# Capped attention, routed experts and a dense layer on one core: cap's terms and the guard's exponential in other places, fewer filling products, and the last tokens' output in two halves of columns

## The chip, the cores and the metric

The kernel runs on one core of a Trainium2 chip. Five engines matter, each with its own queue of instructions, which it works through in order: TensorE (PE) multiplies matrices, VectorE (DVE) and ScalarE (ACT) work on columns, GpSimd (POOL) builds tables and issues indirect DMAs, and SyncE (SP) issues the other DMAs. The engines wait for each other by semaphores. The metric is the device time of one execution in microseconds (us).

## The reference

Three stages follow one another: attention with capped scores, a layer in which each token goes to one of eight experts, and a dense layer with SiLU.

```python
def _attn_ref(q, k, v, cap):                 # 2 batches, 12 heads, 448 tokens, 64 wide
    scores = scale * np.matmul(q, k.transpose(0, 1, 3, 2))
    scores = cap * np.tanh(scores / cap)     # cap = 30
    scores = scores - np.max(scores, axis=-1, keepdims=True)
    attn = np.exp(scores)
    attn = attn / (np.sum(attn, axis=-1, keepdims=True) + 1e-09)
    return np.matmul(attn, v)
...
    logits = x @ w_gate + modality_bias[modality_id]      # 896 tokens, 768 wide, 8 experts
    e_idx = np.argmax(logits, axis=1)
...
        h = np.maximum(x[mask] @ w1[e], 0.0)              # 768 -> 1024
        out[mask] = gate_w[mask, None] * (h @ w2[e])      # 1024 -> 768
...
    h = x @ w_in                                          # 768 -> 2048
    g = h * (1.0 / (1.0 + np.exp(-h)))
    return g @ w_out                                      # 2048 -> 768
```

## The kernel before

**Precision.** Operands of the exact products are split into a high part (fp32r) and the rest, and three products (high by high, rest by high, high by rest) make one. `parts(j)` makes the splits of q and k on DVE.

**Attention.** Heads are worked in 12 pairs. For a pair, `scores(j)` makes the transposed scores in three chunks of 128 keys for both heads and one shared chunk of the last 64 keys of each; ACT takes the tanh out of PSUM (line 339, scaled by `tscale`, which is 0.125 / cap) and then the exp (line 342, scaled by cap). The values of the pair before are multiplied in between (line 402), and their result is copied out of PSUM by ACT (line 412). The row sums are added on DVE (lines 375, 376), moved across partitions by four DMAs on SP's queue (line 385) and folded (lines 391, 392). In the first two pairs, when PE would have nothing to do, `warm(n)` issues n filling products of a zero tile (line 365).

**Cap's terms.** `cap_terms` makes 1/cap, `tscale` (line 187) and an exponent for the guard (line 188) on DVE and issues the DMA of the gate weights on ACT's queue; `cap_guard` makes a flag for a slow path (lines 192, 194) and the guard itself, by an exp of one column on ACT (line 195) and a product on DVE (line 196). The guard is what the softmax adds to its sum; it is first used when pair 0's rows are normalised. Before, both stand behind pair 0's splits and ahead of pair 1's.

**ACT's function table.** The build places an ACT_TABLE_LOAD ahead of the first ACTIVATE whose function is not loaded; one load serves both tanh and exp, and a second comes before SiLU.

**Experts and last layer.** Tokens are sorted by expert, and two experts' weights stream through. The last layer runs in four quarters `q` of the 2048 hidden columns: first the products into the hidden columns (line 1170, SiLU on ACT), then, for seven groups `s` of 128 sorted tokens, 24 products of 128x384 into the 768 output columns (line 1200). For the first five groups the quarters are added up in SBUF (line 1215). The last two groups keep their sums in PSUM through all quarters, one bank for each half of 384 columns; at the end ACT copies one half (line 1210) and DVE the other (line 1211). In the last quarter each group is written by an indirect DMA on POOL's queue (line 1217), with the token rows in `ordr`. The table behind `ordr` is itself made by eight indirect writes (line 892).

**Order.** The code issues each engine's instructions in the order in which it is written (a manual schedule); the framework adds the semaphore waits. `hooks` names what runs after the scores of a pair: 0 is behind pair 0.

Of the kernel before, what the change touches and what calls it, by code (L numbers as in the profile page):

```python
# [13 lines left out]
I32 = mybir.dt.int32  # L14
AF = mybir.ActivationFunctionType
ALU = mybir.AluOpType
# [5 lines left out]
NT, DM, E, FF, DFF = 896, 768, 8, 1024, 2048  # L22
# [10 lines left out]
NQ = 4  # L33
FQ = NFF // NQ
# [28 lines left out]
def moe_stack_kernel(ctx, tc, qT, kT, va, cap, mid, wg, wgb, mb, w1, w2, w_in, w_out, out):  # L63
# [120 lines left out]
    def cap_terms():  # L184
        A.dma_start(out=wg_sb, in_=wgb)
        V.reciprocal(rcap, capt)
        V.tensor_scalar_mul(tscale, rcap, 0.125)
        V.scalar_tensor_tensor(guard, in0=capt, scalar=-1.0, in1=capt, op0=ALU.mult, op1=ALU.min)

    def cap_guard():  # L190
        big = small([1, 1])
        V.tensor_scalar(big, guard[0:1], -CAPMAX, None, op0=ALU.is_lt)
        st["big"], st["slow"] = big, small([1, 1], I32)
        V.tensor_copy(st["slow"], big)
        A.activation(guard, guard, AF.Exp)
        V.tensor_scalar_mul(guard, guard, 1.0e-9)
# [80 lines left out]
    def attention(ap, psa, hooks):  # L277
# [21 lines left out]
        def parts(j):  # L299

            qh, kh = qk["q2", j], qk["k2", j]
            q1 = ap.tile([128, S], F32R, tag="q1", name="q1", bufs=3)
            q3 = ap.tile([128, S], F32R, tag="q3", name="q3", bufs=3)
            k1 = ap.tile([128, KW], F32R, tag="k1", name="k1", bufs=3)
            k3 = ap.tile([128, KW], F32R, tag="k3", name="k3", bufs=3)
            split_t[j] = (q1, q3, k1, k3)

            def first(ks):
                V.tensor_copy(k1[:, ks], kh[:, ks])
                V.tensor_copy(q1, qh)  # L310
                V.tensor_sub(k3[:, ks], kh[:, ks], f32(k1[:, ks]))
                V.tensor_sub(q3, qh, f32(q1[:]))

            if j == 0:
                first(slice(0, 2 * KC))
                V.tensor_copy(k1[:, 2 * KC:], kh[:, 2 * KC:])
                V.tensor_sub(k3[:, 2 * KC:], kh[:, 2 * KC:], f32(k1[:, 2 * KC:]))
            else:
                first(slice(0, KW))
# [161 lines left out]
        load_v(0)  # L481
        load(1)
        parts(0)
        cap_terms()
        cap_guard()
        load(2)
        parts(1)
        for j in range(NP + 2):
            if j + 3 < NP:
                load(j + 3)  # L490
            if j + 1 < NP:
                load_v(j + 1)

            def between():
                if j == NP + 1:
                    warm(6, banks2())
                if j > 1 and not moved(j - 2):
                    rows_of(j - 2)
                if j == 0:
                    warm(8)  # L500
                if j == 1:
                    warm(8)
                if 0 < j <= NP:
                    values(j - 1)
                    evict(j - 1)
                if j == NP:
                    fold(j - 2)
                if 0 < j <= NP:
                    sums(j - 1)
                if j > 1 and j != NP:  # L510
                    fold(j - 2)

            if j < NP:
                scores(j, between)
            else:
                between()
            if j + 2 < NP:
                parts(j + 2)
            for f in hooks.get(2 * j, ()):
                f()  # L520
            if j > 1 and moved(j - 2):
                rows_of(j - 2)
            for f in hooks.get(2 * j + 1, ()):
                f()
# [461 lines left out]
    with (  # L986
        tc.tile_pool(name="attn", bufs=2) as ap,
        tc.tile_pool(name="ps2a", bufs=2, space=PSUM) as ps[2],
        tc.tile_pool(name="psa", bufs=1, space=PSUM) as ps[0],
    ):  # L990
        for _ in range(NWARM):
            T.matmul(bank(), lhsT=wb[:, :128], rhs=wb, start=True, stop=True)
        hooks = {
            0: [setup],
            H + 3: [lambda: choose(0)],
            H + 5: [
                lambda: place(0), lambda: weigh(0, 0), plan_experts, lambda: weigh(0, 1), plan_windows
            ],
            H + 7: [early_window, take_windows, lambda: stream.load(2)],
            H + 8: [do("A", "find", NC), do("A", "gather", 0), do("A", "gather", 1)],  # L1000
            H + 9: [lambda: stream.load(4)],
            H + 10: [do("A", "scale", 0), do("A", "scale", 1), do("A", "flip_both", 0), do("A", "flip_both", 1)],
            H + 11: [lambda: stream.split(1), lambda: stream.load(NLOAD)],
            H + 13: [late_window, lambda: stream.split(2), lambda: stream.load(NF)],
            H + 14: [take_columns],
        }
        attention(ap, ps[0], hooks)
        weigh(1)
# [3 lines left out]
    with tc.tile_pool(name="late", bufs=1) as late:  # L1012
# [142 lines left out]
        osum = late.tile([128, NT // 128, DM], F32, tag="r1", name="osum")  # L1155
        sums = {s: (bank(), bank()) for s in range(NT // 128 - 2, NT // 128)}
        ordr = mo.tile([128, NT // 128, 2], I32, name="ordr")
        for q in range(NQ):
            gs = late.tile([128, 2, FQ, NT], F32R, tag="big", name="gs")
            for fi in range(FQ):  # L1160
                n = 2 * FQ * q + fi
                feed(2 * FQ * q + (4, 5, 6, 8)[fi], 2 * FQ * q + (6, 7, 8, 8)[fi])
                wh, wl = wide.get(n)
                p = banks2()
                i = 0
                for d in range(ND):
                    cs = slice(d * 128, (d + 1) * 128)
                    for w_, x_ in ((wh, 0), (wh, 1), (wl, 0)):
                        for half in range(2):
                            T.matmul(  # L1170
                                p[:, half, :S],
                                lhsT=w_[:, cs],
                                rhs=ys[:, x_, d, half * S:(half + 1) * S],
                                start=(i == 0),
                                stop=(i == 3 * ND - 1),
                            )
                        i += 1
                sg = mo.tile([128, 2, S], F32, tag="tmp", name="sg")
                A.activation(sg, p[:, :, :S], AF.Silu)  # L1179
                sf = sg.rearrange("p a s -> p (a s)")  # L1180
                A.copy(gs[:, 0, fi, :], sf)  # L1181
                V.tensor_sub(gs[:, 1, fi, :], sf, f32(gs[:, 0, fi, :]))  # L1182
            if q == 0:
                plan_order()
                G.dma_start(out=ordr, in_=order.rearrange("(s p) f -> p s f", p=128))
            n = 2 * FQ * q + FQ
            for s in range(NT // 128):
                feed(n + FQ + (0, 0, 0, 1, 1, 2, 2)[s], n + FQ + (0, 1, 2, 2, 3, 3, 4)[s])
                ss = slice(s * 128, (s + 1) * 128)
                held = s in sums  # L1190
                if held:
                    ph = [x[:, :384] for x in sums[s]]
                else:
                    p = banks2()
                    ph = [p[:, half, :384] for half in range(2)]
                for fi in range(FQ):
                    hi, lo = wide.get(n + fi)
                    for i, (g_, w_) in enumerate(((0, hi), (0, lo), (1, hi))):
                        for half in range(2):
                            T.matmul(  # L1200
                                ph[half],
                                lhsT=gs[:, g_, fi, ss],
                                rhs=w_[:, half * 384:(half + 1) * 384],
                                start=(fi == 0 and i == 0 and (q == 0 or not held)),
                                stop=(fi == FQ - 1 and i == 2 and (q == NQ - 1 or not held)),
                            )
                osl = osum[:, s, :].rearrange("p (a c) -> p a c", a=2)
                if held:
                    if q == NQ - 1:
                        A.copy(osl[:, 0], ph[0])  # L1210
                        V.tensor_copy(osl[:, 1], ph[1])  # L1211
                elif q == 0:
                    A.copy(osl, p[:, :, :384])
                else:
                    V.tensor_tensor(out=osl, in0=osl, in1=p[:, :, :384], op=ALU.add)
                if q == NQ - 1:
                    G.indirect_dma_start(  # L1217
                        out=out, out_offset=IOA(ap=ordr[:, s, 0:1], axis=0), in_=osum[:, s, :], in_offset=None
                    )


_OUTS = [((896, 768), "float32")]
# [61 lines left out]
```

## Time and profile before

| | before |
|---|---|
| median of 3 runs | 503.33 us (499.53 to 504.95) |
| the profiled execution, its time | 505.51 us |
| its span, first to last instruction | 503.8 us |
| its mean granted TensorE clock | 0.974 of full speed |
| PE busy | 485.6 us (96%) |
| DVE busy | 322.7 us (64%) |
| ACT busy | 230.9 us (46%) |
| POOL busy | 67.8 us (13%) |

The profile is one execution. Its views show instructions with start and duration in us from the span's start, what ended the idle time before them (in brackets), the time from a DMA's issue to its landing, and in stretches of time the busy time of each engine with the granted TensorE clock, 1.00 for 2.4 GHz and 0.50 for 1.2 GHz. Names left of an arrow are written, names right of it are read; `sc`, `sh`, `p`, `xv` and `out` are accumulators in PSUM.

### The profile page before, as it was taken

To read this page: it belongs to the slowest core of one execution; us is meant where nothing else is said; L and a number is where in the kernel's file an instruction comes from. 1 tells how busy PE (TensorE), PEld (TensorE's weight loads), DVE (VectorE), ACT (ScalarE), POOL (GpSimd) and SP (SyncE) were. 2 spreads that over 40 slices of the span, in tenths; PEclk is the share of its full clock that TensorE was granted. 3 is DMA by queue.
4 is the path that set the end of the run, shared out by engine and by line. 5 is a ranking of instruction groups with operands and counts; after the bars stand their busy time and mean duration, and the time that the engine had idled before them with its cause. 6 is when DMAs were issued, how large, how long until landed. Compare 5 with 4: busy or idle time off the path is not lost.

```text
span 503.8 us, 7670 instructions
## 1 busy us (share of the span) xinstructions
PE 485.6 (96%) x2975; PEld 417.6 (83%) x2975; DVE 322.7 (64%) x554; ACT 230.9 (46%) x275; POOL 67.8 (13%) x151
## 2 busy tenths in 40 slices
PE   8999999989889999999999999999999999999994
PEld 4465666549779988888889999999999999999994
DVE  6679887787647354484777845764877647876220
ACT  5899996921444444243435543354224441235100
POOL 6400006201273300000000011121000000000121
PEclk9999997979789999999999999999999999999999
DMA  7566652832523344735113406685225214340022
GB/s 192 167 172 178 207 168 70 286 89 79 173 74 96 89 119 131 249 134 182 62 64 115 133 6 129 131 125 118 87 103 165 86 62 127 126 126 0 33 94 94
DMA packets 21486, 60.99 MB, mean 121 GB/s; under 512 B 4081, under 2 KB 8689, under 8 KB 21441
## 3 DMA queue, kind: packets, MB, share of 16 engines
q1 hardware_dynamic: 17920, 51.62, 35.6%
q0 software_dynamic: 3088, 8.54, 5.1%
q8 instruction: 25, 0.41, 0.3%
q10 hardware_dynamic: 432, 0.25, 0.2%
q14 instruction: 21, 0.16, 0.1%
HBM read 49.84 MB, written 5.52 MB: 110 GB/s over the span
## 4 chain that ended last, share of the span: by engine, by line
PE 59%; POOLq 0%; issue 0%; DVE 0%
PE sc L1170 23%; PE sc L1200 17%; PE p L1200 7%; PE p L732 6%; PE p L759 6%; POOLq L1280 0%; DVE osum L1211 0%; POOLq L1217 0%
## 5 line engine op out<-in xcount | busy, mean ns | idle before, releaser
L1170 PE MATMUL sc<-ys,hi 128*128 128x448 f32 x384 | 94.4, 368 | 0.0
L1170 PEld LDWEIGHTS sc<-ys,hi 128*128 128x128 f32 x384 | 72.0, 188 | 6.7
L1200 PE MATMUL sc<-hi,gs 128*128 128x384 f32 x320 | 69.1, 336 | 0.0
L1200 PEld LDWEIGHTS sc<-hi,gs 128*128 128x128 f32 x320 | 56.8, 188 | 0.1
L1170 PE MATMUL sc<-ys,lo 128*128 128x448 f32 x192 | 55.0, 367 | 0.0
L125 ACT ACTIVATE w<-raw 128x768 f32<-128x768 f32 x32 | 28.5, 897 | 53.4 <-DVE lo L150 53.4
L759 PE MATMUL p<-r,hi 128*128 128x464 f32 x176 | 51.9, 376 | 0.0
L402 PE MATMUL xv<-at,vx 128*64 128x448 f32 x192 | 43.4, 599 | 0.0
L732 PE MATMUL p<-r,hi 128*128 128x464 f32 (+1 forms) x168 | 41.0, 334 | 0.4 <-PEq L1080 0.4
L1200 PE MATMUL sc<-lo,gs 128*128 128x384 f32 x160 | 40.8, 336 | 0.0
L342 ACT ACTIVATE at<-th,c 128x1344 f32<-128x1344 f32 (+2 forms) x25 | 38.8, 1552 | 0.8
L1170 PEld LDWEIGHTS sc<-ys,lo 128*128 128x128 f32 x192 | 36.0, 188 | 3.4
L339 ACT ACTIVATE th<-sc,c 128x896 f32<-128x896 f32 x36 | 35.1, 1004 | 4.6 <-PE sc L328 4.2
L1182 DVE TENSOR_TENSOR gs<-sg,gs 128x896 fp32r<-128x896 f32 x16 | 17.5, 1092 | 30.8 <-ACT gs L1181 30.8
L759 PEld LDWEIGHTS p<-r,hi 128*128 128x128 f32 x176 | 32.7, 188 | 4.1
L1179 ACT ACTIVATE sg<-sc 128x896 f32<-128x896 f32 x16 | 14.7, 921 | 41.3 <-PE sc L1170 41.3
L149 ACT CAST hi<-w 128x768 fp32r<-128x768 f32 x32 | 26.2, 830 | 16.0 <-DVE w L131 9.4
L402 PEld LDWEIGHTS xv<-at,vx 128*64 128x64 f32 x192 | 13.8, 149 | 23.5 <-issue 22.9
L736 ACT ACTIVATE r<-p 128x256 fp32r<-128x256 f32 (+2 forms) x24 | 10.5, 443 | 49.5 <-PE p L732 35.8
L126 DVE TENSOR_SCALAR w<-w 128x768 f32<-128x768 f32 x32 | 17.9, 558 | 23.9 <-ACT w L125 23.6
L759 PE MATMUL p<-r,lo 128*128 128x464 f32 x88 | 32.9, 374 | 0.0
L328 PE MATMUL sc<-q,k 64*128 64x448 f32 x216 | 30.2, 405 | 2.0 <-ACT th L339 1.9
(237 smaller groups left out, 871.6 us busy)
## 6 DMA issues: line engine op xcount, KB each, us to landing
raw<-in_w_dram SPq DMA_DIRECT2D x32, 384.0 KB, 4.0
raw<-in_w_in_dram SPq DMA_DIRECT2D x16, 768.0 KB, 4.7
raw<-in_w_out_dram SPq DMA_DIRECT2D x16, 768.0 KB, 4.4
gf<-gh SPq DMA_DIRECT2D x44, 112.0 KB, 2.3
vx<-in_va_dram SPq DMA_DIRECT2D x12, 256.0 KB, 4.1
k<-in_kT_dram SPq DMA_DIRECT2D x11, 256.0 KB, 2.9
xd<-xt POOLq DMA_DIRECT2D x6, 448.0 KB, 4.1
q<-in_qT_dram SPq DMA_DIRECT2D x11, 224.0 KB, 2.9
```

The costliest lines, as they stand in the source:

```text
L125: A.activation(w.bitcast(F32), top.bitcast(F32), AF.Abs)
L126: V.tensor_scalar(w.bitcast(F32), w.bitcast(F32), MIN_TOP, None, op0=ALU.max)
L149: A.copy(hi, x)
L328: T.matmul(out[:, :S], lhsT=k_[rows, c * KC:(c + 1) * KC], rhs=q_[rows], start=(i == 0), stop=(i == 2))
L339: A.activation(th[:, c:c + n], p, AF.Tanh, scale=tscale)
L342: A.activation(at[:, c:c + n], th[:, c:c + n], AF.Exp, scale=capt)
L402: T.matmul(p[own, :S], lhsT=vx[:, c * KC + r * D:c * KC + (r + 1) * D], rhs=at[:, 2 * c + r if c < NK else 2 * NK, :], start=(c == 0), sto ...
L732: T.matmul(p[:, :n], lhsT=w_[:, cs], rhs=xs[x_][:, d, :], start=(i == 0), stop=(i == 3 * ND - 1))
L759: T.matmul(p[:, :n], lhsT=w_[:, cs], rhs=hs[h_][:, f, :n], start=(i == 0), stop=(i == 3 * NF - 1))
L1170: T.matmul(p[:, half, :S], lhsT=w_[:, cs], rhs=ys[:, x_, d, half * S:(half + 1) * S], start=(i == 0), stop=(i == 3 * ND - 1),)
L1182: V.tensor_sub(gs[:, 1, fi, :], sf, f32(gs[:, 0, fi, :]))
L1200: T.matmul(ph[half], lhsT=gs[:, g_, fi, ss], rhs=w_[:, half * 384:(half + 1) * 384], start=(fi == 0 and i == 0 and (q == 0 or not held)), ...
```

## The change

Four edits. `cap_terms` moves into `parts(0)`, between the splits that the first two chunks of scores need and those of the other half of k. `cap_guard` moves to the hook behind pair 0's scores, ahead of `setup`. Pair 1's filling products are six instead of eight. The seventh group of tokens makes its 24 products by halves of columns: 12 into the first half, then copies of 192 columns by ACT and by DVE and an indirect write of that half, then the same for the second. The output is seen as 1792 rows of 384 for this, and `ordh` holds the doubled row numbers, made on DVE in quarter 1.

```diff
@@ parts @@
             if j == 0:
                 first(slice(0, 2 * KC))
+                cap_terms()
                 V.tensor_copy(k1[:, 2 * KC:], kh[:, 2 * KC:])
                 V.tensor_sub(k3[:, 2 * KC:], kh[:, 2 * KC:], f32(k1[:, 2 * KC:]))
@@ attention @@
         parts(0)
-        cap_terms()
-        cap_guard()
         load(2)
...
                 if j == 1:
-                    warm(8)
+                    warm(6)
...
         hooks = {
-            0: [setup],
+            0: [cap_guard, setup],
...
+        ordh = mo.tile([128, 2], I32, name="ordh")
...
+            if q == 1:
+
+                V.tensor_scalar(ordh[:, 0:1], ordr[:, NT // 128 - 1, 0:1], 1, None, op0=ALU.logical_shift_left)
+                V.tensor_scalar(ordh[:, 1:2], ordh[:, 0:1], 1, None, op0=ALU.bitwise_or)
...
+                def products(halves):
+                    for fi in range(FQ):
+                        hi, lo = wide.get(n + fi)
+                        for i, (g_, w_) in enumerate(((0, hi), (0, lo), (1, hi))):
+                            for half in halves:
+                                T.matmul(
...
+                def write(to, row, x):
+                    G.indirect_dma_start(out=to, out_offset=IOA(ap=row, axis=0), in_=x, in_offset=None)
+
+                if s == NT // 128 - 1 and last:
+
+                    for half in range(2):
+                        products((half,))
+                        A.copy(osl[:, half, :192], ph[half][:, :192])
+                        V.tensor_copy(osl[:, half, 192:], ph[half][:, 192:])
+                        write(
+                            out.rearrange("t (a c) -> (t a) c", a=2), ordh[:, half:half + 1], osl[:, half]
+                        )
+                    continue
+                products(range(2))
...
                 if q == NQ - 1:
-                    G.indirect_dma_start(
-                        out=out, out_offset=IOA(ap=ordr[:, s, 0:1], axis=0), in_=osum[:, s, :], in_offset=None
-                    )
+                    write(out, ordr[:, s, 0:1], osum[:, s, :])
```

**The order on ACT at the start.** Before, from the first DMA of q to the second tanh; `c` are cap's terms, in brackets the semaphores that each instruction waits for.

```order
L290 DMA q_119<-in_qT_dram 128x448
L292 DMA c_71<-in_cap_dram 128x1
L185 DMA wg_sb<-in_wgb_dram 128x48
L195 ACT_TABLE_LOAD
L195 ACTIVATE c_74<-c_74 128x1 [waits DVE_49]
L339 ACTIVATE th<-sc,c_73 128x896 [waits PE_49]
L342 ACTIVATE at<-th,c_71 128x896 [waits DMAHW3_49,Activation_49]
```

The same place on ACT in the changed program, down to the guard's exp (L195; lines from 314 on are one higher).

```order
L290 DMA q_119<-in_qT_dram 128x448
L292 DMA c_71<-in_cap_dram 128x1
L185 DMA wg_sb<-in_wgb_dram 128x48
L340 ACT_TABLE_LOAD [waits DVE_49]
L340 ACTIVATE th<-sc,c_73 128x896 [waits PE_49]
L343 ACTIVATE at<-th,c_71 128x896 [waits DMAHW3_49,Activation_49]
L340 ACTIVATE th<-sc,c_73 128x896 [waits PE_49]
L343 ACTIVATE at<-th,c_71 128x896 [waits Activation_49]
L340 ACTIVATE th<-sh,c_73 128x448 [waits PE_49]
L340 ACTIVATE th<-sc,c_73 128x896 [waits PE_49]
L343 ACTIVATE at<-th,c_71 128x1344 [waits Activation_49]
L195 ACTIVATE c_74<-c_74 128x1 [waits DVE_49]
```

The guard's exp stands behind pair 0's last exp, and the table load belongs to the first tanh and carries a wait for DVE.

**The order on DVE at the start.** Before, from the last split that pair 0's first chunks need.

```order
L312 TENSOR_TENSOR q_131<-q_119,q_130 128x448 [waits DVE_49]
L316 CAST k_132<-k_118 128x256 [waits DMAHW2_49]
L317 TENSOR_TENSOR k_133<-k_118,k_132 128x256 [waits DVE_49]
L186 RECIPROCAL c_72<-c_71 128x1 [waits DMAHW3_49]
L187 TENSOR_SCALAR c_73<-c_72 128x1 [waits DVE_49]
L188 SCALAR_TENSOR_TENSOR c_74<-c_71 128x1
L192 TENSOR_SCALAR c_144<-c_74 1x1 [waits DVE_49]
L194 CAST c_146<-c_144 1x1 [waits DVE_49]
L196 TENSOR_SCALAR c_74<-c_74 128x1 [waits Activation_49]
```

The same engine in the changed program, a little later: from the end of pair 2's splits to pair 0's sums (L376).

```order
L312 TENSOR_TENSOR q_206<-q_146,q_205 128x448 [waits DVE_49]
L192 TENSOR_SCALAR c_213<-c_74 1x1
L194 CAST c_215<-c_213 1x1 [waits DVE_49]
L196 TENSOR_SCALAR c_74<-c_74 128x1 [waits Activation_49]
L252 TENSOR_SCALAR c_266<-c_265 112x8 [waits Pool_49]
L253 CAST vals<-c_266 112x8 [waits DVE_49]
L252 TENSOR_SCALAR c_266<-c_265 112x8 [waits DVE_49]
L253 CAST vals<-c_266 112x8 [waits DVE_49]
L254 MEMSET vals 112x8
L376 TENSOR_TENSOR gh<-at 128x896
```

Lines 192 to 196 stood right behind cap's terms and now stand behind pair 2's splits; lines 186 to 188 stand directly behind the first L312, ahead of the second half of k.

**The order on POOL at the end.** Before, the writes of the last five groups of tokens; DMASW are the semaphores that tell of the landing of POOL's DMAs, one after another in turn.

```order
L1217 DMA out_dram<-osum,ordr 896x768 [waits DMASW7_49,DVE_49]
L1217 DMA out_dram<-osum,ordr 896x768 [waits DMASW0_49,DVE_49]
L1217 DMA out_dram<-osum,ordr 896x768 [waits DMASW1_49,DVE_49]
L1217 DMA out_dram<-osum,ordr 896x768 [waits DMASW2_49,DVE_49,Activation_49]
L1217 DMA out_dram<-osum,ordr 896x768 [waits DMASW3_49,DVE_49,Activation_49]
```

The changed program, from the third group on.

```order
L1217 DMA out_dram<-osum,ordr 896x768 [waits DMASW7_49,DVE_49]
L1217 DMA out_dram<-osum,ordr 896x768 [waits DMASW0_49,DVE_49]
L1217 DMA out_dram<-osum,ordr 896x768 [waits DMASW1_49,DVE_49]
L1217 DMA out_dram<-osum,ordr 896x768 [waits DMASW2_49,DVE_49,Activation_49]
L1217 DMA out_dram<-osum,ordh 1792x384 [waits DMASW3_49,DVE_49]
L1217 DMA out_dram<-osum,ordh 1792x384 [waits DMASW4_49,DVE_49]
```

The last write has become two of half the columns, and the turn of landing semaphores goes on by one through both.

## Rows read from the trace of the kernel before

**Rows 1.** Chain of waits on the page, shares of the span by line.

```profile
PE sc L1170 23%; PE sc L1200 17%; PE p L1200 7%; PE p L732 6%; PE p L759 6%; POOLq L1280 0%; DVE osum L1211 0%; POOLq L1217 0%
```

**Rows 2.** Timeline of ACT from 0 (start, duration, instruction, [idle before <- releaser]).

```profile
1.24 0.46 ACTq L292 DMA_DIRECT2D c<-in_cap_dram  x1
...
2.22 1.28 ACT L195 ACT_TABLE_LOAD   x1 [2.22 <-issue]
7.28 0.20 ACT L195 ACTIVATE c<-c 128x1 f32<-128x1 f32 x1 [3.78 <-DVE c L192]
7.39 0.99 ACT L339 ACTIVATE th<-sc,c 128x896 f32<-128x896 f32 x1
...
16.27 1.79 ACT L342 ACTIVATE at<-th,c 128x1792 f32<-128x1792 f32 x1
18.83 0.54 ACT L412 COPY xs<-xv 128x448 f32<-128x448 f32 x1 [0.77 <-PE xv L402]
```

**Rows 3.** Timeline of the last 10 us, DVE's last instruction.

```profile
497.14 0.56 DVE L1211 COPY osum<-p 128x384 f32<-128x384 f32 x1 [3.60 <-PE p L1200]
```

**Rows 4.** Timeline of POOL: an order write, the last two output writes.

```profile
299.75 0.98 POOL L892 DMA_INDIRECT order<-ent,order  x1 [2.70 <-DMA order<-ent,order]
...
494.31 0.97 POOL L1217 DMA_INDIRECT out_dram<-osum,ordr  x1 [3.29 <-DVE osum L1211]
498.47 0.97 POOL L1217 DMA_INDIRECT out_dram<-osum,ordr  x1 [3.20 <-DVE osum L1211]
```

**Rows 5.** The output tensor's instructions, the seven writes' time from issue to landing.

```profile
DMA to landing us min/median/max: 3.0/3.0/3.1
```

**Rows 6.** Timeline of DVE in the first 24 us.

```profile
6.00 0.28 DVE L316 CAST k<-k 128x256 fp32r<-128x256 f32 x1
...
6.66 0.16 DVE L186 RECIPROCAL c<-c 128x1 f32<-128x1 f32 x1
6.85 0.15 DVE L187 TENSOR_SCALAR c<-c 128x1 f32<-128x1 f32 x1
...
7.11 0.14 DVE L192 TENSOR_SCALAR c<-c 1x1 f32<-1x1 f32 x1
...
13.58 1.08 DVE L375 TENSOR_TENSOR gh<-at 128x896 f32<-128x896 f32 x1
...
22.93 1.09 DVE L376 TENSOR_TENSOR gh<-gh,at 128x896 f32<-128x896 f32 x1 [3.69 <-ACT at L342]
23.93 0.62 DVE L391 TENSOR_TENSOR gf<-gf,at 128x448 f32<-128x448 f32 x1
```

**Rows 7.** DMA issues: queue, count, KB, us from issue to landing.

```profile
c<-in_cap_dram ACTq DMA_DIRECT2D x1, 0.5 KB, 4.3
```

**Rows 8.** Timeline of ACT, the second table load and what follows it.

```profile
270.82 1.28 ACT L1179 ACT_TABLE_LOAD   x1
272.12 0.92 ACT L1179 ACTIVATE sg<-sc 128x896 f32<-128x896 f32 x1
```

**Rows 9.** Timeline of PE between 12 and 19 us.

```profile
12.90 0.89 PE L328 MATMUL sc<-q,k 64*128 64x448 f32 x6 [1.44 <-ACT th L339]
...
13.73 1.90 PE L365 MATMUL out<-wb 128*128 128x512 bf16 x8
...
15.56 3.23 PE L402 MATMUL xv<-at,vx 128*64 128x448 f32 x16
```

**Rows 10.** Timeline of SP's queue, the moves of pair 0's sums.

```profile
15.89 2.45 SPq L385 DMA_DIRECT2D gf<-gh  x4
```

**Rows 11.** Timeline of DVE in quarter 1, first addition of the output.

```profile
354.80 0.95 DVE L1215 TENSOR_TENSOR osum<-osum,sc 128x768 f32<-128x768 f32 x1 [1.14 <-PE sc L1200]
```

**Rows 12.** Stretches: us, busy PE, PEld, DVE, ACT, POOL, clock, DMA share, GB/s.

```profile
500.00:501.00 1.00, 0.00 (x0) 0.00 (x0) 0.00 (x0) 0.00 (x0) 0.00 (x0) 1.00 0.98 393
```

**Rows 13.** Stretches with the granted clock, columns as above.

```profile
14.00:21.00 7.00, 7.00 (x39) 3.14 (x37) 4.78 (x7) 5.73 (x7) 3.95 (x6) 1.00 0.57 153
75.40:82.00 6.60, 6.60 (x29) 3.56 (x30) 6.05 (x21) 3.80 (x3) 2.76 (x4) 0.50 0.20 55
```

More of the change, by code (lines that the diff above doesn't have):

```diff
@@ L1195, in moe_stack_kernel @@
                     ph = [p[:, half, :384] for half in range(2)]
[L1196 to L1205, printed above, removed]
-                            )
@@ L1207, in moe_stack_kernel @@
-                osl = osum[:, s, :].rearrange("p (a c) -> p a c", a=2)
[L1208 to L1212, printed above, removed]
+                osl = osum[:, s, :].rearrange("p (a c) -> p a c", a=2)
+                last = held and q == NQ - 1
+                def products(halves):
[4 more added lines that the diff above has]
+                                T.matmul(
+                                    ph[half],
+                                    lhsT=gs[:, g_, fi, ss],
+                                    rhs=w_[:, half * 384:(half + 1) * 384],
+                                    start=(fi == 0 and i == 0 and (q == 0 or not held)),
+                                    stop=(fi == FQ - 1 and i == 2 and (q == NQ - 1 or not held)),
+                                )
@@ new lines, in write @@
+                def write(to, row, x):
[7 more added lines that the diff above has]
+                            out.rearrange("t (a c) -> (t a) c", a=2), ordh[:, half:half + 1], osl[:, half]
+                        )
+                    continue
@@ L1213, in moe_stack_kernel @@
+                products(range(2))
+                if last:
+                    A.copy(osl[:, 0], ph[0])
+                    V.tensor_copy(osl[:, 1], ph[1])
+                elif not held and q == 0:
                     A.copy(osl, p[:, :, :384])
-                else:
+                elif not held:
                     V.tensor_tensor(out=osl, in0=osl, in1=p[:, :, :384], op=ALU.add)
                 if q == NQ - 1:
-                    G.indirect_dma_start(
-                        out=out, out_offset=IOA(ap=ordr[:, s, 0:1], axis=0), in_=osum[:, s, :], in_offset=None
-                    )
+                    write(out, ordr[:, s, 0:1], osum[:, s, :])
```

## The prediction

> **What bounds the kernel now.** I read the chain of waits first [rows 1]: it is matmuls to the end, of five lines that are the two experts' and the last layer's products, with DVE and POOL at 0% behind them. So an edit counts only if it moves PE's last product, or what follows it. The change touches two places, the first 20 us and the last 10 us, and I read each from its own timeline.
>
> At the start, ScalarE (ACT) leads. It loads its function table at 2.22, in idle time, computes one column of exp for the guard at 7.28 and starts the first tanh at 7.39; from there it runs without idle time to 18.06 (16.27 + 1.79). Then it waits 0.77 for PE: the eviction of the first pair's values (line 412) starts at 18.83 [rows 2]. That eviction is the point at which I read the sum of the start, since everything after it in the attention is the same loop of PE and ACT, which a shift passes through whole.
>
> At the end, VectorE's (DVE) last copy runs from 497.14 to 497.70, GpSimd's (POOL) last indirect write starts at 498.47, so 0.77 behind the copy, and its bytes land 3.0 later, at 501.47 [rows 3, 4, 5]. The span ends at 503.8, 2.3 after that, and those 2.3 us stay.
>
> **The start, step by step.** The scale of the tanh (line 187) is made on DVE. Before, the second half of pair 0's k splits stood ahead of it; that half began at 6.00 [rows 6]. Now line 186 stands there, if cap has landed: its DMA is issued at 1.24 and takes 4.3, so it is there at 5.5 [rows 2, 7]. Line 187 follows 0.19 later, as it does now (6.66 to 6.85), and takes 0.15: the scale is ready at 6.34, where it is 7.00 now. ACT starts 0.03 after DVE's last step today (line 192 ends at 7.25, ACT starts at 7.28), which gives 6.37.
>
> But the order of the changed program shows more than the diff. The table load is placed directly ahead of the first ACTIVATE. That was the guard's exp, which has one wait, and the load stood free of it. It is now the tanh, which has two waits, for DVE and for PE; the first of them is taken ahead of the load. So the load no longer runs in idle time at 2.22: it starts at 6.37 and lasts 1.28 [rows 2]. The second load of the kernel shows what follows one: 270.82 + 1.28 = 272.10, the ACTIVATE starts at 272.12 [rows 8]. The first tanh so starts at 6.37 + 1.28 + 0.02 = 7.67, **0.28 later** than now, not earlier. The Trainium skill (ScalarE: Activation LUTs, What ACT_TABLE_LOAD costs) gives about 1.28 us for the load and about 1.38 us for a drain with it, 2.66 in all for a switch. By that, the tanh would start at 9.03, ACT would be free at 18.06 + 1.64 + 0.11 = 19.81, the eviction would be about 1.0 late, and the whole sum would be +3.4 instead of +2.2. The trace has no such second part in the 0.02 us between load and ACTIVATE, so I take the 1.28.
>
> The guard's exp moves behind pair 0's last exp. It takes its 0.11 (7.28 to 7.39) there instead, with nothing gained on ACT, which is full: ACT is free at 18.06 + 0.28 + 0.11 = 18.45.
>
> PE's second chunk of pair 1 waits for a tanh at 12.90 [rows 9], so it moves by 0.28 as well. Behind it, the eight filling products run from 13.73 to 15.56, 0.23 each; two fewer are 0.46 less. The values product of pair 0 moves from 15.56 by +0.28 - 0.46 = -0.18, and the eviction from 18.83 to 18.65. ACT is free before that (18.45), so the start as a whole gives **-0.2**. The bounds: -0.46 if the tanh is not late at all, +0.39 (0.28 + 0.11) if the products taken out were hidden anyway.
>
> DVE pays with a stall. Line 196 now waits for that exp. Between it and 18.45 ACT has two tanhs of 0.99 and an exp of 1.79, so it is over at about 14.7. Behind line 196 in DVE's queue stand five small steps of the setup, near 0.15 each, and pair 0's sums, which start at 13.58 now [rows 6]. They start some 2.1 later, at 15.6, and the splits of pair 3 behind them as well. The four moves of the sums on SP's queue, which start at 15.89 and take 2.45, then start at 18.0 [rows 10], with the loads of pair 5 behind them. Nobody is late: DVE stands idle for 3.69 before 22.93, which swallows the 2.1, and the fold that needs the moved sums runs at 23.93 [rows 6], while the moves are issued by 20.5. If that cover were gone it would cost up to 2.1. The k half that now stands behind cap's terms is 0.45 later and is wanted only behind pair 0's filling products. I cost all this at nothing, as the DMA of the gate weights, which keeps its place on ACT's queue.
>
> In the last layer two column steps on DVE make the doubled row numbers, 0.15 each by line 187; DVE has 1.14 of idle time where they stand [rows 11]. Nothing, and 0.3 without that cover.
>
> **The end, step by step.** The 24 products of the last token group are the same 24, each with its own weight load, so PE ends at the same time. The first half is ready half a group earlier (half of the 4.16 us between two writes, so 2.1). Each half is copied in two quarters, and the order shows that DVE's now waits for ACT's; one behind the other I take them as long as the one copy of 0.56 [rows 3].
>
> What decides is the queue behind. Every indirect write into the output waits for the one before it to land: in the order's rows each has one more DMA semaphore among its waits, that of its predecessor. The same form shows in the trace where eight such writes make the order table: POOL idles 2.70 before the second, released by a DMA of the same line [rows 4]. Today it costs nothing, because writes are 4.16 apart (494.31 to 498.47) and take 3.0. With the last group cut in two, it does:
>
> - The sixth group's write starts at 494.31 and lands at 497.31. The first half's data are ready long before, at 497.70 - 2.1 = 495.6, but its write can only start after 497.31. By the 0.77 that POOL takes today behind a release, it starts at 498.08.
> - Half the bytes: the last write's bytes move at 0.98 share in one microsecond [rows 12], so half of them take 0.49 less, and it lands 2.5 after its start, at 500.6.
> - The second half's write waits for that landing, not for its copies (497.7): start 501.36, landing 503.9.
>
> Today's last landing is 501.47. The end gives **+2.4**. The bounds: with no delay behind a release and a landing of 2.0 (no bytes at all) the last landing is 497.31 + 4.0 = 501.3, -0.2; with the longest landing, 3.1, and 0.77 each time it is 505.15, +3.7.
>
> **The sum.** -0.2 + 2.4 = +2.2. On the profiled execution: span 503.8 to 506.0, its time 505.5 to 507.7. That execution lies 2.2 above the median of the runs, 503.33; on the median the forecast is **505.5**, from 503.33 - 0.46 - 0.2 = 502.7 to 503.33 + 0.39 + 3.7 = 507.4.
>
> **The rivals.**
>
> - *The change does what it says*: the load keeps its idle place and the two last writes run side by side. Then the tanh starts at 6.4 at the earliest, 0.99 before now, the eviction 0.99 + 0.46 = 1.45 earlier, and the last write, started at 498.47, lands in 2.5: -0.5. Together -1.9, 501.4. For it speaks only that the diff reads so; both waits stand in the built order. Chance 0.06.
> - *Only the start works*: the load is free of the wait, the writes are not. -1.45 + 2.4 = +1.0, 504.3. Chance 0.08.
> - *The clock falls.* PE's idle time of 1.44 before 12.90 grows by 0.28 to 1.7, and the filling that follows is shorter. Today the granted clock from 14 to 21 us is 1.00 (2.4 GHz); later, from 75.4 to 82.0, it is 0.50 (1.2 GHz) for all of 6.6 us [rows 13]. If such a fall came at 14, PE, which is busy for all of 14 to 21, would do 3.3 us less work in it, and the eviction waits for just that work: +3.3, in all +5.5 and 508.8, slower by 1.1%. It decides from the moment that the stretch reads 0.50. Against it: the present gap did not bring it, and the new one is 0.28 longer. Chance 0.08. The Trainium skill (TensorE: Matmul & The Clock Gate, Part 1) says that the clock follows how busy PE has lately been; the trace agrees in that both levels stand in it.
>
> **How the numbers follow.** The forecast has 0.74; 0.04 is left for what I don't see. A measurement of this kernel can tell about 1%, 5 us, from no change. Slower by over 1% (above 508.4) needs the clock's fall, or the upper bounds together with the spread of the runs, which is 499.53 to 504.95: 0.13. Faster by over 1% (below 498.3) is out of reach of every case but the spread: 0.02. Within 1%: 0.85. The range takes the forecast's own 502.7 to 507.4 and widens it for the spread and toward the clock's fall: 502.0 to 508.3.
>
> **What would show it.** Right: the first table load at about 6.4 instead of 2.2, the first tanh near 7.7, the line 412 eviction near 18.6; the two last writes of POOL near 498.1 and 501.4, the second with idle time ended by a DMA, and a span about 2 us longer, all of it behind PE's last product. Wrong: a load at 2.2 or a tanh before 7; two writes less than 2 us apart; a granted clock of 0.50 between 14 and 21 us.

## The result, and the profile after

Over 19 runs of each, the changed kernel takes 505.49 us (502.45 to 508.19) and the kernel before 501.49 us (499.00 to 504.95): a ratio of 1.0077, with an interval from 1.0054 to 1.0099, so 3.9 us more (2.7 to 5.0). A second set of runs of both kernels gave 1.0079 (1.0045 to 1.0113). The change is slower, by less than 1%. The spread inside each kernel, about 6 us, is larger than the effect. The forecast was 505.5 us, on the median of three runs known then, 503.33; as a difference it was +2.2 us, short of the interval's lower end of 2.7, and a part of what is missing turned out to have a cause of its own.

In the profiles the spread lies ahead of the experts. From 200 to 490 us the granted clock is 1.00 in all fourteen profiles of this case; ahead of that, near 13 us in four of them and else between 75 and 148 us, PE runs at 1.2 GHz for 13.7 to 23.9 us in all, in other stretches each time. So the experts' first products begin at different times even where the code up to them is the same, as in the kernel before and in e11 of the experiments below (start, duration, line, count):

```profile
201.44 30.53 PE p L732 x144
196.83 30.41 PE p L732 x144
```

For this reason the start is read at the first eviction, and what lies behind the attention by its own pieces.

The profiled execution has a span of 506.4 us, 2.6 more than before. Its chain of waits, shares of the span by line, answers to [rows 1]:

```profile
PE sc L1170 23%; PE sc L1208 17%; PE p L1208 7%; PE p L731 6%; PE p L758 6%; DMA out_dram<-osum,ordh 1%; POOLq L1299 0%; DVE osum L1224 0%; ACT osum L1223 0%; POOLq L1217 0%
```

A DMA now stands in the chain, with 1%, and it is a write into the output. The timeline of POOL's last writes answers to [rows 4], and the output's landing times to [rows 5]:

```profile
494.31 0.97 POOL L1217 DMA_INDIRECT out_dram<-osum,ordr  x1 [3.35 <-DVE osum L1232]
498.11 0.97 POOL L1217 DMA_INDIRECT out_dram<-osum,ordh  x1 [2.82 <-DVE osum L1224]
501.44 0.97 POOL L1217 DMA_INDIRECT out_dram<-osum,ordh  x1 [2.36 <-DMA out_dram<-osum,ordh]
```

```profile
DMA to landing us min/median/max: 2.6/3.0/3.0
```

The two halves are written 3.3 us apart, and the idle time ahead of the second is ended by the landing of the first: 498.11 + 2.6 = 500.7. The first half waits for a landing as well, though its row names DVE. DVE's copy that ends just before it, at 497.91, is the second half's; the first half's had ended at 495.80:

```profile
495.44 0.36 DVE L1224 COPY osum<-p 128x192 f32<-128x192 f32 x1 [1.90 <-ACT osum L1223]
```

What held it is the sixth group's write, landed at 494.31 + 3.0 = 497.3, and the write starts 0.8 behind that. From PE's end to the span's end it is 506.4 - 497.18 = 9.22 us, and 503.8 - 497.12 = 6.68 before: +2.54.

The start, on ACT's timeline, answers to [rows 2]:

```profile
6.42 1.28 ACT L340 ACT_TABLE_LOAD   x1 [6.42 <-DVE c L188]
7.71 1.01 ACT L340 ACTIVATE th<-sc,c 128x896 f32<-128x896 f32 x1
...
16.61 1.79 ACT L343 ACTIVATE at<-th,c 128x1792 f32<-128x1792 f32 x1
20.34 0.53 ACT L413 COPY xs<-xv 128x448 f32<-128x448 f32 x1 [1.93 <-PE xv L403]
```

The load is held back to 6.42 and the tanh starts at 7.71, 0.32 late. The eviction is at 20.34, though, not at 18.65. The granted clock of this execution in a stretch of the start tells why, against 1.00 in [rows 13]:

```profile
13.60:16.90 3.30, 2.96 (x11) 1.05 (x8) 2.00 (x8) 3.27 (x5) 1.55 (x6) 0.50 0.66 209
```

On PE's timeline this is most of pair 1's second chunk of scores and the filling products behind it:

```profile
13.24 1.28 PE L329 MATMUL sc<-q,k 64*128 64x448 f32 x6 [1.62 <-ACT th L340]
14.86 2.27 PE L366 MATMUL out<-wb 128*128 128x512 bf16 x5 [0.34 <-issue]
17.06 3.23 PE L403 MATMUL xv<-at,vx 128*64 128x448 f32 x16
```

The values products take 3.23 us as before ([rows 9]), at 2.4 GHz again, but start at 17.06. The experiments show that the fall comes and goes.

One more difference was in no term of the prediction. These rows are pieces of the chain in order of time (start, duration, line, count): quarter 1 of the last layer, before:

```profile
321.04 29.56 PE sc L1170 x144
350.61 20.80 PE sc L1200 x120
371.41 8.32 PE p L1200 x48
```

and after:

```profile
320.34 29.38 PE sc L1170 x144
349.72 21.12 PE sc L1208 x120
370.84 8.44 PE p L1208 x48
```

PE is busy throughout in both, with the same number of the same products. The hidden products take 0.6% less, the output products 1.5% more; a quarter takes 58.94 us instead of 58.68, four of them 1.04 more. The experts' last two stages, of 144 products each, give 0.18 back (30.41 and 30.33 us instead of 30.53 and 30.39), which leaves +0.86.

### The profile page after: what moved, and what is told of

It is laid out like the page before. It is cut to its first block, busy times and chain, and to the rows that moved or that the text cites. A ratio compares the mean times of both kernels' runs of the same rounds, so it can differ in the third digit from the quotient of the medians.

```text
span 506.4 us, 7669 instructions
## 1 busy us (share of the span) xinstructions
PE 484.3 (96%) x2971; PEld 418.2 (83%) x2973; DVE 322.9 (64%) x557; ACT 231.3 (46%) x276; POOL 66.0 (13%) x152
## 4 chain that ended last, share of the span: by engine, by line
PE 59%; DMA 1%; POOLq 0%; issue 0%; DVE 0%; ACT 0%
PE sc L1170 23%; PE sc L1208 17%; PE p L1208 7%; PE p L731 6%; PE p L758 6%; DMA out_dram<-osum,ordh 1%; POOLq L1299 0%; DVE osum L1224 0%; ACT osum L1223 0%; POOLq L1217 0%
## 5 line engine op out<-in xcount | busy, mean ns | idle before, releaser
L403 PE MATMUL xv<-at,vx 128*64 128x448 f32 x192 | 39.6, 556 | 0.0
L150 DVE TENSOR_TENSOR lo<-w,hi 128x768 fp32r<-128x768 f32 x32 | 30.1, 952 | 2.5 <-ACT hi L149 2.5
```

What stands on the lines that cost most here:

```text
L150: V.tensor_sub(lo, x, f32(hi[:]))
L403: T.matmul(p[own, :S], lhsT=vx[:, c * KC + r * D:c * KC + (r + 1) * D], rhs=at[:, 2 * c + r if c < NK else 2 * NK, :], start=(c == 0), sto ...
```

## The experiments

All ratios are to runs of the kernel before that were taken beside them; 0.001 is 0.5 us.

**The two halves of the change, each alone.**

```diff
 # e1_end_only: the changed kernel with the start of before
-                cap_terms()          # in parts(0)
...
+        cap_terms()                  # behind parts(0)
+        cap_guard()
...
-                    warm(6)
+                    warm(8)
...
-            0: [cap_guard, setup],
+            0: [setup],
```

> The last group's output in two halves alone; the start is that of before. Theory: each write into the output waits for the landing of the one before, so POOL's last two writes start at about 498.1 and 501.4 (3.3 apart, the second released by a DMA) and the end costs +2.4 us, a ratio near 1.005. Rival: the writes cost less on average than the one profile shows and most of the 4 us comes from the start: ratio below 1.003. Second rival: the end carries all of it: ratio near 1.008.

Measured: 1.0052 (1.0026 to 1.0078). The last two writes of POOL on its timeline:

```profile
497.61 0.97 POOL L1218 DMA_INDIRECT out_dram<-osum,ordh  x1 [2.82 <-DVE osum L1225]
500.94 0.97 POOL L1218 DMA_INDIRECT out_dram<-osum,ordh  x1 [2.36 <-DMA out_dram<-osum,ordh]
```

They are 3.33 apart, as the theory has it. But this kernel, with the start of before, shows the clock's fall too, in a stretch of its start, and its first eviction comes late:

```profile
12.90:16.20 3.30, 2.97 (x10) 1.57 (x12) 2.91 (x7) 3.27 (x3) 3.13 (x4) 0.50 0.70 224
```

```profile
20.36 0.53 ACT L412 COPY xs<-xv 128x448 f32<-128x448 f32 x1 [2.30 <-PE xv L402]
```

So the fall doesn't need the changed start: with the same start, 18.83 in [rows 2] became 20.36. PE's idle time ahead of pair 1's second chunk, the gap from here on, is another than in [rows 9], though, 1.61 us instead of 1.44:

```profile
12.90 1.49 PE L328 MATMUL sc<-q,k 64*128 64x448 f32 x6 [1.61 <-ACT th L339]
```

```diff
 # e2_start_only: before, with the changed start (cap_terms, cap_guard, six filling products)
```

> Cap's terms, the guard and the six filling products as changed; the end is that of before. Forecast on record: table load at 6.4, first tanh at 7.7, first eviction of a values product near 18.65, -0.2 us, ratio 1.000. Theory after the result: the granted clock falls to 0.50 between about 13.5 and 17, the eviction comes near 20.3, and the change costs about +1.5 us, ratio near 1.003.

Measured: 0.9994 (0.9968 to 1.0021). The clock is 1.00 in its start, and the forecast's numbers come out one by one on ACT's timeline:

```profile
6.42 1.28 ACT L340 ACT_TABLE_LOAD   x1 [6.42 <-DVE c L188]
7.71 1.01 ACT L340 ACTIVATE th<-sc,c 128x896 f32<-128x896 f32 x1
...
18.72 0.53 ACT L413 COPY xs<-xv 128x448 f32<-128x448 f32 x1 [0.31 <-PE xv L403]
```

18.72 where 18.65 was forecast, so -0.1 against 18.83. PE's gap is as long as in the changed kernel, and the values products start 1.61 earlier (15.45 instead of 17.06), which is the price of the fall there:

```profile
13.24 0.87 PE L329 MATMUL sc<-q,k 64*128 64x448 f32 x6 [1.63 <-ACT th L340]
15.45 3.23 PE L403 MATMUL xv<-at,vx 128*64 128x448 f32 x16
```

The theory formed after the result, +1.5 us in this part, falls as an average.

**The parts of the start.**

```diff
 # e3_start_eight: e2 with the eight filling products of before
-                    warm(6)
+                    warm(8)
```

> Cap's terms and the guard moved, but pair 1 keeps its eight filling products; the end is that of before. Table load at 6.4 and first tanh at 7.7 in either theory. If the clock falls because PE's idle time ahead of pair 1's second chunk has grown (1.44 to about 1.6), it falls here as well: the clock reads 0.50 near 14, the eviction is at about 20.8, ratio near 1.004. If it falls because two filling products are gone, it stays at 1.00, the eviction is at about 19.1 and the ratio is within 1.001.

```diff
 # e4_six_only: before, with this alone
-                    warm(8)
+                    warm(6)
```

> Only pair 1's filling products go from eight to six; all else is before. If two products less bring the clock down, it reads 0.50 near 14, the eviction is at about 20, ratio near 1.002 to 1.003. If the longer idle time ahead of them does, the clock stays at 1.00, the eviction is at 18.83 - 0.46 = 18.4 and the ratio is near 0.999.

Measured: 1.0022 (0.9992 to 1.0053) for the moved terms with eight products, 0.9977 (0.9950 to 1.0003) for six products alone. Neither profile has the early fall, though the gap is 1.61 in e3 and 1.55 in e4. The evictions, e3's and e4's, show +0.33 for the later tanh and -0.45 for the two products:

```profile
19.16 0.53 ACT L413 COPY xs<-xv 128x448 f32<-128x448 f32 x1 [0.74 <-PE xv L403]
18.38 0.53 ACT L412 COPY xs<-xv 128x448 f32<-128x448 f32 x1 [0.31 <-PE xv L402]
```

```diff
 # e6_load_early: e3, and an ACTIVATE of one zero element that takes the table load
+    wt = const.tile([1, 1], F32, name="wt")
...
     def cap_terms():
         A.dma_start(out=wg_sb, in_=wgb)
+        A.activation(wt, wb[0:1, 0:1], AF.Tanh)
```

> Before, with cap's terms and the guard moved and a tanh of one zero element ahead of them on ACT, which takes the table load; eight filling products. Theory: the load runs near 2 us in idle time again, the first tanh starts when PE has the first chunk, near 6.8 instead of 7.7, and the first eviction is near 18.2 (18.83 less 0.6); ratio near 0.999. Rival: something else holds the tanh back (cap's DMA, the scale) and it starts at 7.3 or later.

Measured: 0.9981 (0.9957 to 1.0005). ACT's timeline:

```profile
2.22 1.28 ACT L187 ACT_TABLE_LOAD   x1 [2.22 <-issue]
3.51 0.20 ACT L187 ACTIVATE wt<-wb 1x1 f32<-1x1 bf16 x1
6.64 1.01 ACT L342 ACTIVATE th<-sc,c 128x896 f32<-128x896 f32 x1 [2.93 <-PE sc L331]
```

With the load out of the way the tanh waits for PE's first chunk alone and starts 1.07 earlier than in the changed kernel; the eviction comes at 18.08, 0.75 earlier than before. That is what moving cap's terms could have given, and the held-back load took it.

**The end.**

```diff
 # e5_first_half_aside: the changed kernel; the first half goes to another DRAM tensor
+    aside = dram.tile([NT, DM], F32, name="aside")
...
-                            out.rearrange("t (a c) -> (t a) c", a=2), ordh[:, half:half + 1], osl[:, half]
+                            (out if half else aside).rearrange("t (a c) -> (t a) c", a=2), ordh[:, half:half + 1], osl[:, half]
```

> The changed kernel, but the first half of the last group is written to another tensor in DRAM, so 128 x 384 values of the output are left out, and the last write has only the sixth group's write before it, which has landed by then. Theory (the wait for the predecessor's landing is the whole cost of the end): the two writes start near 496.3 and 498.4 instead of 498.1 and 501.4, the last lands at about 501.0, and the kernel is about 2.9 us faster than the changed one, ratio to before about 0.999. Rival (two writes on POOL's queue cost by themselves, by their issue or their fixed time): the last one stays at 500 or later and the ratio stays above 1.003.

Measured: 1.0000 (0.9970 to 1.0030), against 1.0079 for the changed kernel beside it. POOL's timeline:

```profile
494.17 0.97 POOL L1218 DMA_INDIRECT out_dram<-osum,ordr  x1 [3.35 <-DVE osum L1233]
495.93 0.97 POOL L1218 DMA_INDIRECT aside<-osum,ordh  x1 [0.80 <-DVE osum L1225]
498.05 0.97 POOL L1218 DMA_INDIRECT out_dram<-osum,ordh  x1 [1.15 <-DVE osum L1225]
```

Both writes now start on their data, released by DVE, 2.1 apart, and the last one 3.4 us earlier than in the changed kernel. From PE's end (497.03) to the span's end it is 6.0 us, 0.7 less than the 6.68 of before. So two writes close behind one another cost nothing by themselves, and without the wait the split would have paid a little; the wait for the landing of the one before, which a shared output tensor brings, is the cost of the end.

```diff
 # e7_copies_swapped: before, with this alone
-                        A.copy(osl[:, 0], ph[0])
-                        V.tensor_copy(osl[:, 1], ph[1])
+                        V.tensor_copy(osl[:, 0], ph[0])
+                        A.copy(osl[:, 1], ph[1])
```

> Before, with the last two groups' copies exchanged: DVE takes the first half and ACT the second. The write's own wait is for ACT, the waits taken ahead of it are for DVE and the landing. Theory: POOL starts 0.28 behind a release that the write itself waits for, and 0.77 behind one taken ahead of it; ACT ends at about 497.6, the write starts at about 497.9 instead of 498.5, -0.6 us, ratio near 0.999. Rival: the 0.77 belongs to these groups whoever copies last, and the write starts at 498.4 or later, no gain.

Measured: 1.0003 (0.9970 to 1.0036). DVE's last copy, and POOL's write:

```profile
496.34 0.56 DVE L1210 COPY osum<-p 128x384 f32<-128x384 f32 x1 [3.60 <-PE p L1200]
```

```profile
497.67 0.97 POOL L1217 DMA_INDIRECT out_dram<-osum,ordr  x1 [3.19 <-ACT osum L1211]
```

```profile
496.51 0.48 ACT L1211 COPY osum<-p 128x384 f32<-128x384 f32 x1 [3.68 <-PE p L1200]
```

DVE ends at 496.90, and the write starts 0.77 behind that, though its row names ACT, which ends at 496.99. Of the expected 0.6 us only about 0.15 is there: DVE now takes the half whose products end first (its copy starts 0.17 ahead of ACT's), but its copy is the longer one, and the wait for it, taken ahead of the write, is still followed by 0.77.

**The changed kernel again.**

```diff
 # e9_after_again: no edit
```

> The changed kernel once more, on the chip of the other runs of this call. By the sum of its two parts measured alone (1.0052 and 0.9994) the ratio is near 1.005, +2.3 us. If the parts work on each other it stays near 1.0077 as first measured. Its profile shows whether the early fall of the clock is there each time.

Measured: 1.0079 (1.0045 to 1.0113). The parts alone give 1.0052 and 0.9994, so 1.0046 together, inside this run's interval but at its lower end. The early fall of the clock is there again, from 13.2.

**The products.** In the built program the new tile of row numbers takes 32 bytes of each partition and moves all tiles of the late pool by as much: ys (moving operand of line 1170) and gs (weights of line 1200). The splits hi and lo, which meet both, stay. The distance in a partition from hi and lo to ys and gs, as a remainder by 128 bytes, is 96 before and 0 after.

```diff
 # e10_rows_wider: the changed kernel with
-        ordh = mo.tile([128, 2], I32, name="ordh")
+        ordh = mo.tile([128, 16], I32, name="ordh")
```

> The changed kernel with the tile of doubled row numbers 16 wide instead of 2, so that the late tiles move by another 32 bytes in each partition. Theory: the last layer's products differ by 1% because the new tile moved the late operands (gs, ys) by 32 bytes against the weights' splits (hi, lo); here the distance is again that of before, so 120 output products take 20.80 us instead of 21.12 and 144 hidden products 29.56 instead of 29.37, and the kernel is about 0.9 us faster than the changed one: ratio to before about 1.005. Rival: the products are slower because of the code around them; then they stay at 21.12 and 29.37 and the ratio near 1.008.

```diff
 # e11_shift_only: before, with this alone
+        pad = mo.tile([128, 2], I32, name="pad")
+        V.memset(pad, 0)
```

> Before, with a tile of two columns that nobody reads at the place of the doubled row numbers; it moves the late operands by 32 bytes and does nothing else. Theory: 120 output products take 21.12 us and 144 hidden products 29.37, so the last layer is about 0.9 us longer, ratio about 1.002. Rival: nothing changes, 20.80 and 29.56.

```diff
 # e12_two_shifts: e11, and between r2 (which ys takes over) and the tiles that gs follows
+        gap = late.tile([128, 8], I32, name="gap")
+        V.memset(gap, 0)
```

> As the run before, and a second unread tile of 32 bytes between ys and gs: ys stands as in the changed kernel, gs as in before. Theory: each operand has its own effect, so the hidden products take 29.37 and the output products 20.80, about 0.9 us less than before, ratio about 0.998. Rival: it is one effect of all late tiles together, and the products take either pair of times or others.

Measured: 1.0062 (1.0029 to 1.0094), 1.0013 (0.9983 to 1.0043) and 1.0006 (0.9975 to 1.0038), all too wide for a microsecond. The pieces of the chain don't vary from quarter to quarter, and they decide. e11, quarter 1:

```profile
316.51 29.38 PE sc L1172 x144
345.89 21.12 PE sc L1202 x120
```

An unread tile at that place brings exactly the changed kernel's pair of times, so neither the code nor the order of the products does it. e10 and e12, the same quarter:

```profile
315.69 28.82 PE sc L1170 x144
344.51 21.20 PE sc L1208 x120
```

```profile
318.66 29.37 PE sc L1174 x144
348.03 21.20 PE sc L1204 x120
```

e10, with 64 bytes more than before, was expected back at 29.56 and 20.80: a miss, and so was e12's 20.80. By the remainder of the distance all kernels fall in line: 144 hidden products take 29.56 us at 96 (before), 29.37 at 0 (after, e11, e12) and 28.82 at 32 (e10); 120 output products take 20.80 at 96, 21.12 at 0 and 21.20 at 32 (e10, e12). In e6 another early tile moved hi, lo, ys and gs by 32 together, and its pair is that of before, so it is the distance that counts:

```profile
318.23 29.56 PE sc L1171 x144
347.80 20.80 PE sc L1201 x120
```

A remainder of 64 was not tried.

**A version that should beat both.**

```diff
 # e13_best: e6, e4, e7 and e12 together
```

> A version that should beat both: one output write for the last group with ACT copying last, cap's terms and guard moved as in the change, a tanh of one element that takes the table load early, six filling products, and the two distances of the run before. Sum by what was measured in profiles: first eviction 1.1 us earlier, last write 0.5 to 0.6 earlier, products 0.9 less: -2.6 us, ratio about 0.995. Rival: what is won at the start is lost in the stretches in which the clock falls; then the ratio is about 0.997.

Measured: 1.0002 (0.9971 to 1.0033): no gain. Its profile shows why. The eviction is at 17.85, so -1.0 where -1.1 was expected. The end gains about 0.15, as in e7, and not 0.5 to 0.6. And its distances are those of e12, taken before e12's times were known, with output products of 21.20: a quarter takes 59.05 us instead of 58.68, four 1.5 more, and less the 0.18 it is +1.3. The sum is +0.2. The version that the rows point to, e6's start with ys at the remainder 32 and gs at 96, was not run.

## Why the prediction was right, and what it missed

- *The table load held back, the tanh late*: right. 6.42 and 7.71, forecast 6.37 and 7.67, though the diff looks like a gain there. The choice of 1.28 for the load, without a second part, was right as well: the tanh follows the load by 0.01.
- *The start as a whole, -0.2*: right by -0.1 where the clock stays up (e2), and the ratio 0.9994 agrees. In the changed kernel's own profile it was +1.5, because the rival of the clock's fall, to which 0.08 was given, did occur there: 0.50 from 13.60 to 16.90, which is one of the prediction's own signs of being wrong. Its mechanism, a gap that grows from 1.44 to 1.7, is borne out in part. All four falls (the two profiles of the changed kernel, e1, e5) came behind a gap of 1.61 to 1.63, and none behind the shorter gaps of five other profiles (0.97 to 1.55); but e2, e3, e7, e10 and e12 have the same 1.61 to 1.63 without a fall. Nor does the change alone make the gap: with the start of before it lay between 1.44 and 1.62, from one execution to the next. The fall was also dearer on paper than here: 3.3 us for a fall of 6.6, 1.6 for this one of about 3.3 (20.34 against 18.72). That a shift of the first eviction passes to the end whole, as the prediction took it, is not shown: the experts begin up to 4.6 us apart with the same start (201.44 and 196.83).
- *DVE's stall behind the guard's exp, at nothing*: right. Pair 0's sums started at 15.66 (forecast 15.6) and at 15.55 in e2, whose next second sum still stood behind idle time and started at 22.82, where [rows 6] have 22.93:

```profile
15.66 1.08 DVE L376 TENSOR_TENSOR gh<-at 128x896 f32<-128x896 f32 x1
22.82 1.09 DVE L377 TENSOR_TENSOR gh<-gh,at 128x896 f32<-128x896 f32 x1 [2.29 <-ACT at L343]
```

- *The end, +2.4*: right, +2.54. The two writes started at 498.11 and 501.44 where 498.1 and 501.4 were forecast, the half landed in 2.6 instead of 2.5, and e5 shows the cause by taking it away.
- *The change does what it says*, and *only the start works*: both out, the first by the 3.3 us between the writes, the second by the load at 6.42. Their 1.45 for a free load was too much besides: e13, with the load early and six products, gained 0.98, since the tanh then waits for PE's first chunk.
- *The term that failed* is "Nothing" for the two column steps of the row numbers. The steps themselves are hidden, as forecast. Their tile is not: it moved the last layer's operands by 32 bytes, and that costs +0.86.

The sum of what was measured in profiles is -0.1 + 0.86 + 2.54 = +3.3 us, in both intervals of the ratio, where the forecast had +2.2. What is left to +3.9 is 0.6. It may be noise. Or the early fall may come more often with the changed start: it stands in three of the five profiles that have it whole (the two of the changed kernel and e5, not e2 and e10) and in one of the nine others (e1), and it costs 1.5 to 1.6 each time. With it, as in the changed kernel's own profile, the sum would be 1.5 + 0.86 + 2.54 = +4.9. For it speaks that all six profiles with the late tanh have the gap of 1.61 to 1.63, and only three of the six with the start of before (e1, e7, e12). These are too few to tell, and this stays open. That the time itself came out at 505.5 owes something to luck: the difference was too small by 1.7 and the three runs of before, from which it was counted, lay 1.8 too high.

## What to carry to other kernels

Look in the built order for what a moved instruction carries. Here the first ACTIVATE carries the table load, and where it has two waits, one of them comes ahead of the load. A split write carries a wait for the landing of the one before, where this program writes both into one tensor, so pieces pay only if each lands before the next has its data. And when a tile is added, look at where it pushes the operands of the products that bound the kernel: a microsecond went that way here without a single instruction of them changed.

## What the runs showed of the hardware that was not expected

- The time of back-to-back fp32r products of 128x448 and 128x384 depends on the distance between the two operands in a partition: 28.82 to 29.56 us for 144, 20.80 to 21.20 us for 120, by the remainder of the distance by 128 bytes, and the best distance for one is not the best for the other. Why is not shown.
- The fall of the granted clock near 13 us came in four of fourteen profiles, in kernels with either start, and cost 1.5 to 1.6 us each time. PE had stood idle for 1.61 to 1.63 us ahead of it, but the same idle time went without a fall in e2, e3, e7, e10 and e12.
- A release that is taken ahead of an indirect write, rather than by the write's own wait, is followed by 0.77 us before POOL starts it (DVE's copy in e7, 496.90 to 497.67; the landing in the changed kernel, 500.67 to 501.44); where DVE's release was the write's own wait, it was 0.28 (e5: 497.77 to 498.05).
